# One expert layer, a second buffer for the w2 combinations, the fifth expert's raw sums in SBUF, folding from item 19, attention copies ahead of the weight cast

## The chip, the cores and the metric

One core of one Trainium2 chip. The metric is the device time of one execution in microseconds; the figure before is the median of three runs. TensorE (PE) multiplies and loads weights (PEld), VectorE is DVE, ScalarE is ACT, GpSimd is POOL, and SyncE (SP) issues every DMA of this kernel, all on one queue.

## The reference, cut to what matters

```python
x = chunked_attention(q, k, v)            # 2304 tokens x 512, chunks of 64
P = sinkhorn(exp(x @ w_gate - max))       # 2304 x 8, 8 rounds of row and column norm
for e in range(8):                        # every expert sees every token
    h = relu(x @ w1[e])                   # 512 -> 1024
    out += P[:, e:e+1] * (h @ w2[e])      # 1024 -> 512
h = max(out @ w1, out @ w2, out @ w3)     # second layer, 512 -> 768, with relu
return h @ w_out
```

P is known only when all tokens have been through the attention and the Sinkhorn rounds are over.

## The kernel before, in words

Each fp32 product is made of three matmuls of rounded high and low parts. The tokens are three blocks of 768. The first layer runs over 32 pairs of 128-wide weight blocks per token block ("items" 0 to 31 for block 0, 32 to 63 and 64 to 95 for the others), four items to an expert; the second layer has 27 short items. An item has seven steps (pos 0 to 6), and each step is one Strassen-like product of 6 matmuls into one of three PSUM banks: `pa` (pos 0, 2, 4, 6), `pg` (pos 1 and 5) and `pb` (pos 3). Banks accumulate over the steps of an item.

In block 0 the weights come raw from the inputs. While item n runs, the weight combinations of item n+1 are made for w1 (`prep`, pos 0 and 1) and those of item n for w2 (`prep`, `prep_x`, pos 2 to 5), by ACT (rounding casts), POOL and DVE (remainders). They are used at once and also stored to DRAM (`keep`): the w1 combinations to `w1s` (1792 KB an item, L193), the w2 ones to `w2s` in four stores, of which the two combinations that only later blocks need are `w2x` (L198) and `w2y` (L200), 512 KB each. `w2x` is one place in SBUF (two slots of `wr`) and `w2y` one tile, both reused by every item: the cast that begins the next `w2x` (L182) waits until the store of the last one has landed. Behind L182 and the `w2y` cast (L247) in ACT's queue stand the relu's of pos 4 to 6 (L273), behind the relu of pos 5 stands DVE's remainder (L279), the last reader of bank `pg`, and pos 1 of the next item writes `pg`.

After pos 1, 3 and 5 two down projections of the item before run on PE (L444, 12 matmuls), so an item of block 0 has 42 up and 36 down matmuls. DVE or ACT evicts them. For block 0 the sums of experts 0 to 4 (NRAW = 5) are kept raw: four items into `ar`, then `ar` stored to `up_part` in DRAM, as P is not known. From expert 5 on `ar` takes P-scaled sums, and `fold_all` loads the 30 raw tiles of 256 KB again (`u`, L496) and adds them scaled to `ar` (L499 on DVE), four an item, from item 22.

The attention of the last 12 token tiles is spread over items 0 to 13: scores at pos 6, normalisation at pos 1, values (`att_pv`) at pos 0 of the next item, its copies out of PSUM (L772, PSUM pool `dn`, shared with the down projections) behind ACT's weight cast L247 of that pos; then the store `x_save` at pos 2 and `gate` at pos 4, which takes a buffer of pool `pa` and is evicted by L783. From item 32 on the weights come back from `w1s` and `w2s` through a ring of slots in `wr`.

The order of everything is the order of the code: a table `bg[(n, pos)]` of callbacks (`at`) runs after the step's product, and `prep` runs ahead of the table. SP issues in program order; an issue whose buffer is not free holds all later ones.

Of the kernel before, what the change touches and what calls it, by code (L numbers as in the profile page):

```python
# [9 lines left out]
F32 = mybir.dt.float32  # L10
F32R = mybir.dt.float32r
# [3 lines left out]
AF = mybir.ActivationFunctionType  # L15
ALU = mybir.AluOpType
AX = mybir.AxisListType

P = 128
# [3 lines left out]
DM = H * D  # L23
# [6 lines left out]
KD = DM // P  # L30
SB = 3
TS = NT // SB
W = TS * P // 2
# [5 lines left out]
NRAW = 5  # L39
# [13 lines left out]
def kernel(ctx: ExitStack, tc: tile.TileContext, qk, vv, wg, wts, wts2, out):  # L53
    nc = tc.nc
# [6 lines left out]
    rp = raws.enter_context(tc.tile_pool(name="raw", bufs=1, side="right"))  # L61
# [21 lines left out]
    ar = rg.tile([P, TS, DM], F32, name="ar")  # L83
    xs = dram.tile([NT, P, KD, P], F32, name="xs")
    ys = dram.tile([NT, P, KD, P], F32, name="ys")
    up_part = dram.tile([NRAW, TS, P, DM], F32, name="upart")
    scr = dram.tile([3 * NP2, P, 7, 2, 2, P], F32, name="scr")
    scro = dram.tile([NP2, P, 2, 2, DM], F32, name="scro")
    w1s = dram.tile([NPAIR, P, 7, 512], F32, name="w1s")
# [46 lines left out]

    w1b = lambda n: wr[:, 7 * (n % 2):7 * (n % 2) + 7]
    w2b = lambda n: wr[:, 14 + 4 * (n % 2):18 + 4 * (n % 2)]
    w2x = wr[:, 22:24]

    def prep(n, step):
        if not own(n):
# [15 lines left out]
    def prep_x(n, step):  # L158

        if not own(n):  # L160
            return
        q = lambda c, a: sw[n][:, c].rearrange("p (f a k r) -> p a k f r", a=2, k=2, f=4)[:, a]
        o = lambda x: x.rearrange("p (k f r) -> p k f r", k=2, f=4)
        tt = nc.vector.tensor_tensor
        if step == 0:
            p = wk.tile([P, 2, 256], F32, name="xw", tag="wk")
            s = rp.tile([P, 2, 256], F32, name="w2c", tag="w2c")
            sw2[n] = (p, s)
            for a in range(2):
                nc.scalar.copy(out=o(p[:, a]), in_=q(0, a))  # L170
        elif step == 1:
            p, s = sw2[n]
            w = w2b(n)[:, 0:2]
            tt(out=w[:, :, 1], in0=p, in1=w[:, :, 0].bitcast(F32), op=ALU.subtract)
            tt(out=o(s[:, 0]), in0=q(1, 1), in1=o(p[:, 1]), op=ALU.add)
            tt(out=o(p[:, 1]), in0=q(0, 0), in1=o(p[:, 1]), op=ALU.subtract)
            tt(out=p[:, 0], in0=s[:, 0], in1=p[:, 0], op=ALU.subtract)
            tt(out=o(s[:, 1]), in0=q(1, 0), in1=o(p[:, 0]), op=ALU.subtract)
            sw.pop(n)
        elif step == 2:  # L180
            p, s = sw2[n]
            nc.scalar.copy(out=w2x[:, :, 0], in_=p)  # L182
            y = sums["y", n] = rp.tile([P, 2, 2, 256], F32R, name="w2y", tag="w2y")
            hilo(y[:, :, 0], y[:, :, 1], s)
        else:
            p, s = sw2.pop(n)
            tt(out=w2x[:, :, 1], in0=p, in1=w2x[:, :, 0].bitcast(F32), op=ALU.subtract)

    def keep(n, step):
        f32 = lambda x: x.bitcast(F32).rearrange("p s h f -> p s (h f)")  # L190
        w2o = w2s[n // 2, :, :, n % 2]
        if step == 0:
            nc.sync.dma_start(out=w1s[n], in_=f32(w1b(n)))  # L193
        elif step == 1:
            nc.sync.dma_start(out=w2o[:, 0:1], in_=f32(w2b(n)[:, 0:1]))
            nc.sync.dma_start(out=w2o[:, 5:7], in_=f32(w2b(n)[:, 2:4]))
        elif step == 2:
            nc.sync.dma_start(out=w2o[:, 2:4], in_=f32(w2x))  # L198
        else:
            nc.sync.dma_start(out=w2o[:, 1:5:3], in_=f32(sums.pop(("y", n))))  # L200

# [246 lines left out]
    def new_acc(t):  # L448
        acc[t] = ar[:, t % TS]
        return acc[t]  # L450

    def evict(it, t, p):
        e, pp = it["e"], it["pp"]
        raw = it["sb"] == 0 and e < NRAW
        if raw or it["g"] == 0 or (it["sb"] == 0 and e == NRAW and pp == 0):
            if pp == 0:
                a = new_acc(t)
                if raw:
                    nc.scalar.copy(out=a, in_=p)
                else:  # L460
                    nc.scalar.activation(out=a, in_=p, func=AF.Copy, scale=Pt[:, t, e:e + 1])
            else:
                nc.vector.tensor_tensor(out=acc[t], in0=p, in1=acc[t], op=ALU.add)
                if pp == 3:
                    nc.sync.dma_start(out=up_part[e, t], in_=acc[t])
            return
        nc.vector.scalar_tensor_tensor(
            out=acc[t], in0=p, scalar=Pt[:, t, e:e + 1], in1=acc[t], op0=ALU.mult, op1=ALU.add)
        if it["g"] == NPAIR - 1:
            y_due.append((clock[0], t))  # L470

# [10 lines left out]
    def y_out(t):  # L482
        p = wk.tile([P, KD, P], F32, name="yp", tag="wk")
        for k in range(KD):
            nc.tensor.transpose(p[:, k], acc[t][:, k * P:(k + 1) * P], ident)
        y = acc[t].rearrange("p (k q) -> p k q", k=KD)
        nc.scalar.copy(out=y, in_=p)
        nc.sync.dma_start(out=ys[t], in_=y)

    def fold_all():  # L490
        jobs = [(e, t) for e in range(NRAW) for t in range(TS)]
        got = {}
        for i in range(len(jobs) + 5):
            if i < len(jobs):
                got[i] = big[0].tile([P, DM], F32, name="u", tag="ld", bufs=6)
                nc.sync.dma_start(out=got[i], in_=up_part[jobs[i]])  # L496
            if i >= 5:
                e, t = jobs[i - 5]
                nc.vector.scalar_tensor_tensor(out=acc[t], in0=got.pop(i - 5), scalar=Pt[:, t, e:e + 1],  # L499
                                               in1=acc[t], op0=ALU.mult, op1=ALU.add)  # L500
            yield


    xst = {}

    def x_load(k):
        kind, sb = phases[k]
        if k == 1:
            T = lambda i: big[0].tile([P, 2, W], F32, name=f"xf{i}", tag=f"xf{i}")
        else:  # L510
            T = lambda i: bg_[:, :7 * 2 * W].rearrange("p (i a w) -> p i a w", a=2, w=W)[:, i]
        xst.update({i: T(i) for i in range(7)})
        for i, (q, h) in {5: (1, 0), 0: (0, 0), 2: (1, 1), 1: (0, 1)}.items():
            for j in range(TS // 2):
                t, o = sb * TS + 2 * j + q, xst[i][:, :, j * P:(j + 1) * P]
                nc.sync.dma_start(out=o, in_=(xs if kind == "M" else ys)[t, :, 2 * h:2 * h + 2])
                yield
# [162 lines left out]
    def load_v(t):  # L680
        if t < NT:
            v_t[t] = ap_.tile([P, DM], F32, name="v", tag="v", bufs=3)
            nc.sync.dma_start(out=v_t[t], in_=vv[t])
# [90 lines left out]
    def x_save(t):  # L774
        nc.sync.dma_start(out=xs[t], in_=raw_of(t))
# [56 lines left out]
                              in_=pts[sb - 1, :, q, e].partition_broadcast(P))  # L832


    bg = {}

    def at(n, pos, fn):
        bg.setdefault((n, pos), []).append(fn)
# [5 lines left out]
        at(n, 2, lambda t=t: att_swap(t))  # L844
    for m in range(NT - NPE):
        t, n = NPE + m, 1 + m
        at(n + 1, 0, lambda t=t: (att_pv(t, dn), load_v(t + 3)))
        at(n + 1, 2, lambda t=t: x_save(t))
        at(n + 1, 4, lambda t=t: gate(t, ps_a))
    for t in range(NPE):  # L850
        at(t // 2, 3 + 2 * (t % 2), lambda t=t: gate(t, wk))
    n = NT - NPE + 2
# [13 lines left out]
    def att_close():  # L866
        nonlocal pbm
        att.close()
        pbm = pool("pbm").tile([P, 2, 2, W], F32, name="pbm")
        big[0] = bigs.enter_context(tc.tile_pool(name="big", bufs=1))  # L870

    pbm = bg_ = tq = None
    s3, sr, bigr = ExitStack(), ExitStack(), [None]
# [23 lines left out]

    at(n, 0, att_close)
    for g in range(NPAIR):
        for s_, (a, b) in enumerate(((0, 0), (0, 6), (1, 1), (1, 1))):  # L900
            at(g + a, b, lambda g=g, s_=s_: keep(g, s_))
    decs, folds = [decode_all(i) for i in range(2)], fold_all()

# [4 lines left out]

    for i in range(2):
        at(first_of[2 + i] - 5, 6, lambda i=i: [None for _ in decs[i]])  # L910
    f0 = 4 * NRAW + 2
    for i in range(NRAW * TS + 5):
        at(f0 + i // 4, (0, 2, 4, 6)[i % 4], lambda: next(folds, None))
    for k in range(1, 4):
        n0 = first_of[k]
        g = x_load(k)
        for i in range(13):
            at(*((n + 1 + i // 4, i % 4) if k == 1 else (n0 - 4, i // 2)), lambda g=g: next(g, None))
        for step_ in range(4):
            at(*((n + 5 + step_ // 2, 2 * (step_ % 2)) if k == 1 else  # L920
                 (n0 - 2 + step_ // 3, step_ % 3)), lambda s_=step_: x_sums(s_))
        for pos in range(7) if k == 1 else (0, 2):
            a = 7 * (n0 - 1) + pos + 1
            at(a // 7, a % 7, lambda pos=pos: x_put(pos, 0))
            at((a + 1) // 7, (a + 1) % 7, lambda pos=pos, k=k: x_put(pos, 1, k > 1))
# [21 lines left out]
    with tc.manual_schedule():  # L947
# [43 lines left out]
        for n in range(ni):  # L991
# [3 lines left out]
            for pos in up(n):  # L995
                clock[0] = 7 * n + pos
                if y_due and y_due[0][0] < 7 * n + pos - 1:
                    y_out(y_due.pop(0)[1])
                if pos < 2:
                    prep(n + 1, pos)  # L1000
                elif pos == 2:
                    prep(n, 2)
                    prep_x(n, 0)
                elif pos == 5:
                    prep_x(n, 3)
# [85 lines left out]
```

## Time and profile before

| what | before |
|---|---|
| median of three runs | 1831.68 us (1830.63 to 1832.98) |
| profiled execution | 1831.47 us, its span 1829.7 us |
| PE busy / PEld busy | 1796.5 us / 1704.8 us |
| DVE, ACT, POOL busy | 1314.0, 781.1, 999.3 us |
| DMA | 537.36 MB, 82.6% of 16 engines' span on SP's queue |
| mean granted PE clock | 0.995 of full speed |

PE is nearly always busy, so what counts is where it is not. A matmul's end is modelled in this profile, and neighbours overlap in the rows: six up matmuls start some 1.05 us before the next piece does. Times are from the start of the span; block 0 ends at about 620 us.

### The profile page before, as it was taken

The numbers are of one execution on the slowest core, as the hardware profiler recorded it, in microseconds if no ns is written. First come the engines' busy times: TensorE is split into PE (matmuls) and PEld (weight loads), VectorE is DVE, ScalarE is ACT, GpSimd is POOL, SyncE is SP. The second block draws the span as 40 slices with busy tenths as digits, with TensorE's granted clock in tenths as the row PEclk, the third lists the DMA queues.
The fourth block names the chain that finished last, engine by engine and source line by source line (L and its number), as shares of the span: only waits on it lengthen the run. The fifth ranks groups of instructions, "written<-read, shape, count | busy, mean of one in ns | idle before, by whom it ended". The sixth has DMA issues, their size and how long they took to land.

```text
span 1829.7 us, 30169 instructions
## 1 busy us (share of the span) xinstructions
PE 1796.5 (98%) x10734; PEld 1704.8 (93%) x10740; DVE 1314.0 (72%) x2344; ACT 781.1 (43%) x1574; POOL 999.3 (55%) x894
## 2 busy tenths in 40 slices
PE   7999999999999899999999999999999999999999
PEld 5888888988888899999999999999999999999998
DVE  7666675775887577877888677878888767655535
ACT  5555555555544443343333344333433333333221
POOL 6554555677765667666676577657676655000000
PEclk9999999999999999999999999999999999999999
DMA  6798987989998788989888878988889896877663
GB/s 243 262 342 325 333 303 286 354 316 345 360 333 320 278 308 305 315 285 321 294 312 292 298 273 302 317 287 305 316 308 305 263 319 244 268 254 253 244 248 114
DMA packets 207415, 537.36 MB, mean 294 GB/s; under 512 B 15936, under 2 KB 94880, under 8 KB 182048
## 3 DMA queue, kind: packets, MB, share of 16 engines
q1 hardware_dynamic: 207264, 535.43, 82.6%
q8 instruction: 85, 1.39, 0.3%
q14 instruction: 66, 0.54, 0.1%
HBM read 376.19 MB, written 157.60 MB: 292 GB/s over the span
## 4 chain that ended last, share of the span: by engine, by line
PE 83%; DMA 7%; DVE 4%; issue 2%; ACT 2%; SPq 1%; POOL 1%; POOLq 0%; DVEq 0%; ACTq 0%
PE pa L328 24%; PE dn L386 24%; PE dn L444 14%; PE pg L328 12%; PE pb L328 6%; DMA w2s<-w2y 4%; DMA w2s<-wr 1%; DMA u<-upart 1%; PE gp L782 1%; DMA w1s<-wr 1%; PE s L693 1%; PE xp L770 0%; DVE s L702 0%; DVE hr L279 0%; ACT hr L273 0%
## 5 line engine op out<-in xcount | busy, mean ns | idle before, releaser
L328 PE MATMUL pa<-xh,wr 128*128 128x384 f32 x1824 | 538.8, 338 | 2.9 <-ACT s L335 1.0
L444 PE MATMUL dn<-wr,hr 128*128 128x512 f32 x1476 | 360.2, 395 | 2.6 <-ACT xr L772 2.5
L328 PEld LDWEIGHTS pa<-xh,wr 128*128 128x128 f32 x1824 | 336.1, 188 | 9.5 <-ACT s L335 1.9
L444 PEld LDWEIGHTS dn<-wr,hr 128*128 128x128 f32 x1476 | 276.5, 189 | 60.1 <-ACT xr L772 5.8
L328 PE MATMUL pa<-xl,wr 128*128 128x384 f32 x912 | 306.5, 336 | 2.6 <-DVE xl L541 2.6
L328 PE MATMUL pg<-xh,wr 128*128 128x384 f32 x912 | 274.4, 341 | 12.5 <-DVE hr L279 11.7
L386 PE MATMUL dn<-hr,wr 128*128 128x384 f32 x1344 | 274.2, 334 | 0.0
L335 ACT COPY s<-pa 128x384 f32<-128x384 f32 x246 | 118.6, 482 | 300.5 <-PE pa L328 262.2
L386 PEld LDWEIGHTS dn<-hr,wr 128*128 128x128 f32 x1344 | 236.8, 188 | 0.1
L341 DVE TENSOR_TENSOR c<-pb,s 128x384 f32<-128x384 f32 x82 | 45.7, 558 | 205.7 <-PE pb L328 173.2
L248 POOL TENSOR_TENSOR hr<-c,hr 128x384 fp32r<-128x384 f32 x96 | 110.7, 1159 | 146.0 <-ACT hr L247 140.4
L328 PEld LDWEIGHTS pg<-xh,wr 128*128 128x128 f32 x912 | 168.9, 189 | 16.8 <-DVE hr L279 15.0
L386 PE MATMUL dn<-hx,wr 128*128 128x384 f32 x840 | 180.3, 334 | 0.6 <-DVE ar L395 0.6
L328 PEld LDWEIGHTS pa<-xl,wr 128*128 128x128 f32 x912 | 171.5, 188 | 6.8 <-issue 2.9
L328 PE MATMUL pg<-xl,wr 128*128 128x384 f32 x456 | 153.4, 337 | 0.0
L386 PEld LDWEIGHTS dn<-hx,wr 128*128 128x128 f32 x840 | 148.7, 188 | 1.2 <-DVE ar L395 1.2
L248 POOL TENSOR_TENSOR hr<-tq,hr 128x384 fp32r<-128x384 f32 x128 | 148.2, 1174 | 0.0
L248 POOL TENSOR_TENSOR w2y<-w2c,w2y 128x512 fp32r<-128x512 f32 x32 | 41.6, 1301 | 175.3 <-ACT w2y L247 150.7
L328 PE MATMUL pb<-xh,wr 128*128 128x384 f32 x456 | 134.4, 335 | 0.0
L248 POOL TENSOR_TENSOR hx<-c,hx 128x384 fp32r<-128x384 f32 x60 | 68.5, 1144 | 108.2 <-ACT hx L247 107.0
L395 DVE TENSOR_TENSOR ar<-dn,ar 128x384 f32<-128x384 f32 x240 | 122.6, 546 | 6.8 <-PE dn L386 6.8
L386 PE MATMUL dn<-hy,wr 128*128 128x384 f32 x504 | 111.0, 335 | 0.5 <-DVE ar L395 0.5
(189 smaller groups left out, 3313.3 us busy)
## 6 DMA issues: line engine op xcount, KB each, us to landing
wr<-w2s SPq DMA_DIRECT2D x80, 1024.0 KB, 6.2
w1s<-wr SPq DMA_DIRECT2D x32, 1792.0 KB, 9.1
wr<-w1s SPq DMA_DIRECT2D x54, 1024.0 KB, 7.5
wr<-w1s SPq DMA_DIRECT2D x59, 768.0 KB, 6.8
w2s<-wr SPq DMA_DIRECT2D x64, 512.0 KB, 8.3
wr<-w2s SPq DMA_DIRECT2D x52, 512.0 KB, 6.5
wr<-scr SPq DMA_DIRECT2D x22, 1024.0 KB, 5.0
wr<-scr SPq DMA_DIRECT2D x27, 768.0 KB, 5.8
```

The lines of the kernel that those rows point to most:

```text
L248: (eng or nc.gpsimd).tensor_tensor(out=l, in0=v, in1=h.bitcast(F32), op=ALU.subtract)
L328: nc.tensor.matmul(ps, lhsT=wt[:, x, ws], rhs=y[:, xi, k], start=b not in begun, stop=k == 1 and i == 2, skip_group_check=True)
L335: nc.scalar.copy(out=s[pos], in_=ps)
L341: nc.vector.tensor_tensor(out=inner, in0=ps, in1=s[other], op=ALU.add)
L386: nc.tensor.matmul(p, lhsT=w[:, a, dt * P:(dt + 1) * P], rhs=h[m][:, b], start=m == 0 and q == 0, stop=m == 1 and q == 2)
L395: nc.vector.tensor_tensor(out=o, in0=p, in1=o, op=ALU.add)
L444: nc.tensor.matmul(o, lhsT=h[:, hi, ts], rhs=w, start=(f == 0 and i == 0), stop=(f == 1 and i == 2))
L693: nc.tensor.matmul(ss[g][cs, hp, :], lhsT=a[r, hp, 0, cs], rhs=a[r, hp, 1, cs], start=True, stop=True)
L782: nc.tensor.matmul(p, lhsT=x[:, k, :], rhs=wgr[:, k, :], start=k == 0, stop=k == KD - 1)
```

## The change

- A second place `w2z` for both `w2x` and `w2y` is opened with the pool `big` at item 14; odd items from 15 on use it.
- The stores of `w2x` and `w2y` of item n move from pos 1 to pos 0 of item n+1, and there ahead of the 1792 KB store of `w1s`.
- The raw sums of the fifth expert (e = 4) go to a tile `spare` in SBUF, not to DRAM: 24 stores and 24 loads where there were 30 each.
- `ar` is first written by an ACT copy with P as its scale (six tiles of expert 0, items 19 and 20), then folding adds expert 4 from `spare`, then experts 1 to 3; three jobs an item from item 19, none at pos 4 on DVE. Expert 5's first sums are added by DVE where ACT wrote them.
- The loads of block 1's tokens (`x_load`) move from items 15 to 18 to items 22 to 26, four of their seven tiles lie in `spare`; their sums (`x_sums`) move to items 29 and 30.
- `att_pv` runs ahead of `prep` (table `early`), and `gate` moves from pos 4 to pos 2.

```diff
-    up_part = dram.tile([NRAW, TS, P, DM], F32, name="upart")
+    up_part = dram.tile([NRAW - 1, TS, P, DM], F32, name="upart")
...
-    w2x = wr[:, 22:24]
+    w2z = []
+    w2x = lambda n: w2z[0][:, 0:2] if w2z and n % 2 else wr[:, 22:24]
...
             p, s = sw2[n]
-            nc.scalar.copy(out=w2x[:, :, 0], in_=p)
-            y = sums["y", n] = rp.tile([P, 2, 2, 256], F32R, name="w2y", tag="w2y")
+            x = w2x(n)
+            sums["x", n] = x
+            nc.scalar.copy(out=x[:, :, 0], in_=p)
+            y = w2z[0][:, 2:4] if w2z and n % 2 else rp.tile([P, 2, 2, 256], F32R, name="w2y", tag="w2y")
+            sums["y", n] = y
             hilo(y[:, :, 0], y[:, :, 1], s)
...
-        raw = it["sb"] == 0 and e < NRAW
-        if raw or it["g"] == 0 or (it["sb"] == 0 and e == NRAW and pp == 0):
+        if e < NRAW:
+            a = spare[0][:, t] if e == NRAW - 1 else ar[:, t]
             if pp == 0:
-                a = new_acc(t)
-                if raw:
-                    nc.scalar.copy(out=a, in_=p)
-                else:
-                    nc.scalar.activation(out=a, in_=p, func=AF.Copy, scale=Pt[:, t, e:e + 1])
-            else:
-                nc.vector.tensor_tensor(out=acc[t], in0=p, in1=acc[t], op=ALU.add)
-                if pp == 3:
-                    nc.sync.dma_start(out=up_part[e, t], in_=acc[t])
+                nc.scalar.copy(out=a, in_=p)
+                return
+            nc.vector.tensor_tensor(out=a, in0=p, in1=a, op=ALU.add)
+            if pp == 3 and e < NRAW - 1:
+                nc.sync.dma_start(out=up_part[e, t], in_=a)
             return
...
-        jobs = [(e, t) for e in range(NRAW) for t in range(TS)]
+        jobs = [(e, t) for e in (0, NRAW - 1, *range(1, NRAW - 1)) for t in range(TS)]
+        loads = [j for j in jobs if j[0] != NRAW - 1]
         got = {}
...
+        def load():
+            if loads and len(got) < 6:
+                e, t = loads.pop(0)
+                got[e, t] = big[0].tile([P, DM], F32, name="u", tag="ld", bufs=6)
+                nc.sync.dma_start(out=got[e, t], in_=up_part[e, t])
+
+        for _ in range(5):
+            load()
+        yield
+        for e, t in jobs:
+            load()
+            if e == 0:
+                nc.scalar.activation(out=ar[:, t], in_=got.pop((e, t)), func=AF.Copy, scale=Pt[:, t, e:e + 1])
+            else:
+                u = spare[0][:, t] if e == NRAW - 1 else got.pop((e, t))
+                nc.vector.scalar_tensor_tensor(out=ar[:, t], in0=u, scalar=Pt[:, t, e:e + 1],
+                                               in1=ar[:, t], op0=ALU.mult, op1=ALU.add)
             yield
...
-        at(n + 1, 0, lambda t=t: (att_pv(t, dn), load_v(t + 3)))
-        at(n + 1, 2, lambda t=t: x_save(t))
-        at(n + 1, 4, lambda t=t: gate(t, ps_a))
+        early[n + 1, 0] = lambda t=t: (att_pv(t, dn), load_v(t + 3))
+        at(n + 1, 2, lambda t=t: (x_save(t), gate(t, ps_a)))
...
+        spare.append(big[0].tile([P, TS, DM], F32, name="spare"))
+        w2z.append(big[0].tile([P, 4, 2, 256], F32R, name="w2z"))
...
-        for s_, (a, b) in enumerate(((0, 0), (0, 6), (1, 1), (1, 1))):
+        for s_, (a, b) in enumerate(((0, 0), (0, 6), (1, 0), (1, 0))):
             at(g + a, b, lambda g=g, s_=s_: keep(g, s_))
...
-    f0 = 4 * NRAW + 2
-    for i in range(NRAW * TS + 5):
-        at(f0 + i // 4, (0, 2, 4, 6)[i % 4], lambda: next(folds, None))
+    at(n + 4, 5, lambda: next(folds))
+    for i in range(NRAW * TS):
+        at(n + 5 + i // 3, (0, 2, 4 + 2 * (i >= TS))[i % 3], lambda: next(folds, None))
...
-            at(*((n + 1 + i // 4, i % 4) if k == 1 else (n0 - 4, i // 2)), lambda g=g: next(g, None))
+            at(*((n + 8 + i // 5 + 2 * (i >= 9), i % 5) if k == 1 else (n0 - 4, i // 2)),
+               lambda g=g: next(g, None))
...
+                if (n, pos) in early:
+                    early[n, pos]()
                 if pos < 2:
                     prep(n + 1, pos)
```

In the changed kernel the source lines are numbered otherwise (L193 is L198 there, L198 is L203, L200 is L205, L182 is L185, L273 is L278, L772 is L788). On SP's queue, at the start of item 28, after the loads of the raw weights `st`, there stood:

```order
L119 DMA st<-in_wts 128x512
L120 DMA st<-in_wts 128x2x256
L193 DMA w1s<-wr 128x3584
L496 DMA u<-upart 128x512
L198 DMA w2s<-wr 128x2x512
L200 DMA w2s<-w2y 128x2x512
```

and in the changed kernel, at the same place:

```order
L119 DMA st<-in_wts 128x512
L120 DMA st<-in_wts 128x2x256
L203 DMA w2s<-w2z 128x2x512
L205 DMA w2s<-w2z 128x2x512
L198 DMA w1s<-wr 128x3584
L847 DMA pbm<-pts 128x3x128 x2
```

The two stores of item 27's combinations now come from `w2z` and stand ahead of the `w1s` store, and no `u` load is left here.

On ACT, at the start of an attention item (`s<-pa` and `s<-pg` are the copies behind pos 0 and pos 1, `xr<-xp` those of the attention values), before:

```order
L703 ACTIVATE s<-s 128x256 x2
L335 COPY s_2770<-pa 128x384
L247 CAST wr<-st 128x3x256
L772 COPY xr<-xp 128x4x64 x2
L335 COPY s_2811<-pg 128x384
```

and now:

```order
L719 ACTIVATE s<-s 128x256 x2
L340 COPY s_2770<-pa 128x384
L788 COPY xr<-xp 128x4x64 x2
L252 CAST wr<-st 128x3x256
L340 COPY s_2813<-pg 128x384
```

The two copies change places with the cast.

On ACT in item 19 of the changed kernel, from the cast that begins the odd item's `w2x` to the relu of pos 6:

```order
L185 CAST w2z<-xw 128x2x256
L252 CAST w2z<-w2c 128x2x256
L278 ACTIVATE hr<-c 128x384
L280 ACTIVATE c<-c 128x384
L508 ACTIVATE ar<-u,Pt 128x512
L278 ACTIVATE hr<-pg 128x384
```

where before stood:

```order
L182 CAST wr<-xw 128x2x256
L247 CAST w2y<-w2c 128x2x256
L273 ACTIVATE hr<-c 128x384
L275 ACTIVATE c<-c 128x384
L273 ACTIVATE hr<-pg 128x384
```

The casts have another target, and a scaled copy of expert 0 stands ahead of the relu of pos 5.

## Rows read from the trace of the kernel before

**Rows 1.** The page: the span, and busy time by engine.

```profile
span 1829.7 us, 30169 instructions
PE 1796.5 (98%) x10734; PEld 1704.8 (93%) x10740; DVE 1314.0 (72%) x2344; ACT 781.1 (43%) x1574; POOL 999.3 (55%) x894
```

**Rows 2.** Busy time in stretches: engines, granted clock, DMA share, GB/s.

```profile
450.00:500.00 50.00, 48.83 (x241) 43.20 (x240) 42.63 (x67) 24.43 (x49) 34.98 (x28) 1.00 0.98 366
500.00:550.00 50.00, 48.53 (x241) 43.15 (x240) 42.18 (x68) 25.45 (x50) 36.11 (x28) 1.00 0.96 340
550.00:600.00 50.00, 43.71 (x209) 38.44 (x207) 32.94 (x55) 21.71 (x44) 24.59 (x18) 0.95 0.84 328
650.00:700.00 50.00, 50.00 (x290) 50.00 (x289) 37.64 (x63) 22.71 (x47) 36.47 (x37) 1.00 0.89 301
```

**Rows 3.** Waits of PE over the span: us in total, times, longest.

```profile
PE pg L328 <- DVE hr L279: 11.7, 8, 4.8
...
PE dn L444 <- ACT xr L772: 2.5, 4, 0.9
...
PE pa L328 <- ACT Pt L783: 0.8, 2, 0.6
```

**Rows 4.** Waits of ACT over the span, those of L182 on DMA.

```profile
ACT wr L182 <- DMA w2s<-wr: 73.8, 17, 7.3
```

**Rows 5.** Timeline of ACT, items 29 and 30: start, duration, idle before.

```profile
559.62 0.59 ACT L182 CAST wr<-xw 128x512 fp32r<-128x512 f32 x1 [7.26 <-DMA w2s<-wr]
560.85 0.62 ACT L247 CAST w2y<-w2c 128x512 fp32r<-128x512 f32 x1 [0.64 <-DMA w2s<-w2y]
...
563.45 0.86 ACT L247 CAST wr<-st 128x768 fp32r<-128x768 f32 x1
...
576.99 0.59 ACT L182 CAST wr<-xw 128x512 fp32r<-128x512 f32 x1 [3.83 <-DVE w2c L178]
```

**Rows 6.** Chain that ended last, in order of time: start, us, piece.

```profile
230.07 3.02 PE dn L444 x12
...
549.69 1.04 PE pb L328 x6
...
563.47 1.34 PE pg L328 x6
564.81 4.33 PE dn L444 x12
...
571.22 2.76 PE dn L444 x12
...
601.51 2.29 PE pg L328 x6
603.79 3.64 PE dn L444 x12
```

**Rows 7.** Busy time in stretches behind the two longest waits, columns as rows 2.

```profile
563.00:567.00 4.00, 3.53 (x12) 3.07 (x13) 3.17 (x5) 1.79 (x4) 3.92 (x5) 0.71 0.99 417
601.00:605.00 4.00, 3.49 (x10) 3.20 (x11) 1.58 (x3) 3.29 (x6) 4.00 (x4) 0.50 1.01 394
```

**Rows 8.** Timeline of SP's queue, item 28: start and duration of an issue.

```profile
547.03 0.37 SPq L193 DMA_DIRECT2D w1s<-wr  x1
...
549.06 0.87 SPq L198 DMA_DIRECT2D w2s<-wr  x1
```

**Rows 9.** Line L198 (stores of w2x), 440 to 600 us: issue to landing.

```profile
DMA to landing us min/median/max: 9.3/10.0/14.7
```

**Rows 10.** Line L193 (stores of w1s), 440 to 580 us: issue to landing.

```profile
DMA to landing us min/median/max: 8.9/10.3/11.0
```

**Rows 11.** Timeline of ACT at the start of an attention item.

```profile
228.90 0.84 ACT L247 CAST wr<-st 128x768 fp32r<-128x768 f32 x1
229.63 0.66 ACT L772 COPY xr<-xp 128x256 f32<-128x256 f32 x2
```

**Rows 12.** The page, DMA issues: KB each, median us to landing.

```profile
u<-upart SPq DMA_DIRECT2D x30, 256.0 KB, 8.8
```

More of the change, by code (lines that the diff above doesn't have):

```diff
@@ L186, in prep_x @@
             p, s = sw2.pop(n)
-            tt(out=w2x[:, :, 1], in0=p, in1=w2x[:, :, 0].bitcast(F32), op=ALU.subtract)
+            x = sums["x", n]
+            tt(out=x[:, :, 1], in0=p, in1=x[:, :, 0].bitcast(F32), op=ALU.subtract)
     def keep(n, step):
@@ L197, in keep @@
         elif step == 2:
-            nc.sync.dma_start(out=w2o[:, 2:4], in_=f32(w2x))
+            nc.sync.dma_start(out=w2o[:, 2:4], in_=f32(sums.pop(("x", n))))
         else:
@@ L453, in evict @@
         e, pp = it["e"], it["pp"]
-        raw = it["sb"] == 0 and e < NRAW
-        if raw or it["g"] == 0 or (it["sb"] == 0 and e == NRAW and pp == 0):
+        if e < NRAW:
+            a = spare[0][:, t] if e == NRAW - 1 else ar[:, t]
             if pp == 0:
-                a = new_acc(t)
-                if raw:
-                    nc.scalar.copy(out=a, in_=p)
-                else:
-                    nc.scalar.activation(out=a, in_=p, func=AF.Copy, scale=Pt[:, t, e:e + 1])
-            else:
-                nc.vector.tensor_tensor(out=acc[t], in0=p, in1=acc[t], op=ALU.add)
-                if pp == 3:
-                    nc.sync.dma_start(out=up_part[e, t], in_=acc[t])
+                nc.scalar.copy(out=a, in_=p)
[3 more added lines that the diff above has]
+                nc.sync.dma_start(out=up_part[e, t], in_=a)
             return
         nc.vector.scalar_tensor_tensor(
-            out=acc[t], in0=p, scalar=Pt[:, t, e:e + 1], in1=acc[t], op0=ALU.mult, op1=ALU.add)
+            out=ar[:, t], in0=p, scalar=Pt[:, t, e:e + 1], in1=ar[:, t], op0=ALU.mult, op1=ALU.add)
         if it["g"] == NPAIR - 1:
@@ L484, in y_out @@
         for k in range(KD):
-            nc.tensor.transpose(p[:, k], acc[t][:, k * P:(k + 1) * P], ident)
-        y = acc[t].rearrange("p (k q) -> p k q", k=KD)
+            nc.tensor.transpose(p[:, k], ar[:, t, k * P:(k + 1) * P], ident)
+        y = ar[:, t].rearrange("p (k q) -> p k q", k=KD)
         nc.scalar.copy(out=y, in_=p)
@@ L490, in fold_all @@
     def fold_all():
-        jobs = [(e, t) for e in range(NRAW) for t in range(TS)]
+        jobs = [(e, t) for e in (0, NRAW - 1, *range(1, NRAW - 1)) for t in range(TS)]
+        loads = [j for j in jobs if j[0] != NRAW - 1]
         got = {}
[L493 to L500, printed above, removed]
+        def load():
[14 more added lines that the diff above has]
+                                               in1=ar[:, t], op0=ALU.mult, op1=ALU.add)
             yield
+    spare = []
     xst = {}
@@ L508, in x_load @@
         if k == 1:
-            T = lambda i: big[0].tile([P, 2, W], F32, name=f"xf{i}", tag=f"xf{i}")
+            xf = spare[0].rearrange("p t d -> p (t d)").rearrange("p (i a w) -> p i a w", a=2, w=W)
+            T = lambda i: (xf[:, (1, 3, 4, 6).index(i)] if i in (1, 3, 4, 6) else
+                           big[0].tile([P, 2, W], F32, name=f"xf{i}", tag=f"xf{i}"))
         else:
@@ L832, in p_load @@
                               in_=pts[sb - 1, :, q, e].partition_broadcast(P))
-    bg = {}
+    bg, early = {}, {}
     def at(n, pos, fn):
@@ L917 @@
         for i in range(13):
-            at(*((n + 1 + i // 4, i % 4) if k == 1 else (n0 - 4, i // 2)), lambda g=g: next(g, None))
+            at(*((n + 8 + i // 5 + 2 * (i >= 9), i % 5) if k == 1 else (n0 - 4, i // 2)),
+               lambda g=g: next(g, None))
         for step_ in range(4):
-            at(*((n + 5 + step_ // 2, 2 * (step_ % 2)) if k == 1 else
+            at(*((n + 15 + step_ // 2, 2 * (step_ % 2)) if k == 1 else
                  (n0 - 2 + step_ // 3, step_ % 3)), lambda s_=step_: x_sums(s_))
```

## The prediction

> **What bounds the kernel now.** I read the page first, then busy time in stretches, then the waits of PE and of ACT, then the timelines around the longest waits, and last the chain. PE is busy 1796.5 of 1829.7 us [rows 1], so at most 33 us can be won without less PE work, and the change removes no matmul. From 650 us on, in the later blocks, PE is busy all of a stretch at full clock [rows 2]: time won before is kept to the end. What PE lacks in block 0's second half is 1.17, 1.47 and 6.29 us in three stretches of 50 us [rows 2], while the DMA engines are 98, 96 and 84% busy. The list of waits names the cause: PE waits 11.7 us in 8 pieces, the longest 4.8, for DVE's remainder L279 to let go of bank `pg`, and 3.3 us in 6 pieces in the attention items for ACT's copies L772 and L783 [rows 3].
>
> L279 is only the last link. In ACT's queue the relu that it needs stands behind L182, and L182 waited for the store of the last `w2x` 17 times, 73.8 us in all [rows 4]. In item 29 it began at 559.62 after 7.26 us, and the `w2y` cast behind it had 0.64 us more to wait; in item 30, where the store was in time, ACT was idle 3.83 us until DVE had made the input [rows 5]. So 3.83 us is what that place costs anyway, and the store made item 29 about 3.4 us worse; PE's `pg` then began at 563.47 [rows 6].
>
> **The change part by part.**
>
> *Second buffer, earlier stores.* The store of `w2x` takes 9.3 to 14.7 us to land, median 10.0 [rows 9], and in item 28 it was issued 2.0 us behind the 1792 KB store of `w1s` [rows 8]. Odd items from 15 now write `w2z`, even ones a place last read two items ago, some 31 us, against at most 14.7 us of landing. L182 and the cast behind it then wait for DVE alone, as in item 30, and all eight `pg` waits should go: 11.7 us [rows 3].
>
> A wait costs more than its idle time. Six matmuls behind one take 1.34 us on the chain against 1.04 [rows 6]: 0.30 more, times 8, is 2.4 us.
>
> Two waits also cost clock. Before the wait that ended at 563.47 and the one that ended at 601.51 the clock was at its full level, 2.4 GHz; behind them the stretch means were 0.71 and 0.50 of it, the latter being 1.2 GHz [rows 7]. Twelve down matmuls took 4.33 and 3.64 us there instead of 2.76, and the six ahead of the second 2.29 instead of 1.34 [rows 6]: 1.57 + 0.88 + 0.95 = 3.4 us, which come back with the waits.
>
> *Attention.* The copies L772 stood behind a cast; the row behind the cast's start begins 0.73 us later [rows 11]. That covers most of the longest such wait, 0.9 us, and the four together are 2.5 us [rows 3]. Moving `gate` to pos 2 puts its copy L783 ahead of L182, which ends the other 0.8 us. Refilling PE costs 0.26 a wait here (3.02 against 2.76 for twelve down matmuls [rows 6]), 1.6 for six. Bounds: 4.9 us if all goes, nothing if something else in ACT's queue holds the copies as long; with the `w2x` stores landing earlier too I take 4.0, near the upper end, because both waits stand directly behind what is moved away.
>
> *The fifth expert in SBUF.* Six stores and six loads of 256 KB fall away, 3.1 MB, no PE time by themselves. DVE's count of folds falls from 30 to 24, but six first sums of expert 5 come to it from ACT, so DVE is even. What helps is that pos 4, where DVE has L279's chain, has no fold now: counted at nothing, since item 30 with one there had no wait.
>
> *Six scaled copies on ACT.* They are new on the path that ends in L279. A cast of the same 128x512 size takes 0.59 us [rows 5]. Two of the six stand between L182 and the relu of pos 5 (items 19 and 20); the first may also wait for its load, whose landing took 8.8 us in the median [rows 12]. It is issued only at pos 5 of the item before, behind the `sw` load, so up to some 4 us late, but there ACT holds only copies that PE needs from pos 4 on, 6 us later. Bounds 0 and 0.6 x 2 + 1; I take 1.0 us as loss. Behind the first copy on ACT stands the weight cast of pos 1, for which POOL waits; POOL is 55% busy [rows 1] and takes that.
>
> *Later `x_load`, `x_sums`.* The sums stand in items 29 and 30 where two folds stood; `spare` is read by folds until item 22 and loaded from item 25, so no wait. In item 31 the casts of block 1's tokens share ACT with the relu's; by the times behind L182 there PE would be late by 0.1 to 0.5 us, taken as 0.2.
>
> *`w1s` stores behind the pair.* 1 MB more is ahead of them, at 340 GB/s [rows 2] 3.1 us. Their landing of 8.9 to 11.0 us [rows 10] becomes 12 to 14. The cast that overwrites their source came 16.4 us after the issue in item 28 (547.03 [rows 8], 563.45 [rows 5]), 13.0 without the 3.4 us of that item's wait. So the cast may come up to 1 us late in the worst item. ACT's idle time before L182, 3.83 us [rows 5], covers that: nothing now, up to 1 us an item if that cover is gone.
>
> *Pace of the DMA engines.* By the sizes in the code an item moves 4.72 MB, with four `u` loads 5.77, with three 5.51; items 23 and 26, with `x_load` beside, 5.8 and 5.9. Undisturbed an item is 3 x 2.76 + 7 x 1.05 = 15.6 us [rows 6], which asks for 353 to 377 GB/s; the rows show 366 over 50 us [rows 2] and 394 to 417 over 4 us [rows 7]. I count nothing for it: an excess of 3% over two items is half a microsecond an item, less than any slack above. The Trainium skill, page "DMA: Bandwidth & Descriptors", section "Specifications", gives about 358 GB/s as the HBM limit of a core. The stretch at 366 does not agree with it as a ceiling; by it items 23 and 26 would run 0.5 and 0.9 us over and the sum would be 1.4 us higher.
>
> *Sum.* 11.7 + 2.4 + 3.4 + 4.0 - 1.0 - 0.2 = 20.3 us. The profiled execution took 1831.47 us, 1.8 more than its span, and the median of the runs is 1831.68, so no correction is due: 1831.5 - 20.3 = **1811.2 us**.
>
> **The rivals.**
>
> A. The transfers become the bound and one wait replaces the other. For it: shares of 96 to 98% [rows 2]. If the engines yield 340 GB/s and no more, an item of 5.5 to 5.9 MB needs 16.2 to 17.3 us, and loads of raw weights come late instead of stores. Then what PE lacked from 450 to 600 us, 8.9 us, stays: 1820.1. Against it: ACT's list shows no wait of its weight casts for loads, and less is moved than before. The rule of about 358 GB/s named above points this way; the 366 of the rows speaks against it.
>
> B. The attention part gives nothing, because the copies are held by the scores' exponentials ahead of them: 1815.2.
>
> C. The buffer does not matter, since DVE is the real holder of L182 (it was in item 30). Then only the attention part comes, less the losses: 1828.7. Against it: item 30 waited for DVE and PE did not wait for `pg` afterwards.
>
> D. Slower: the `w1s` store, now behind 1 MB more, holds the cast at pos 0 in every item, at 1 us of PE for each us beyond ACT's idle time. To turn a gain of 20.3 into a loss over 31 items it must exceed that by 0.65 us an item, so land 13.0 + 3.8 + 0.65 = 17.5 us after issue against my 12 to 14; at 18.5 us it would give 1842. Against it: the longest landing now is 11.0.
>
> **How the numbers follow.** Main case 0.60, A 0.15, B 0.14, C 0.06, D 0.05. The forecast is the main case's. Without the losses and with the whole attention part it is 1809.1, and waits too short for the list may add some 2 us (an estimate): 1807 is the lower end. The upper end takes in B and A: 1821. About 0.2% (3.7 us) is what a measurement here can tell from no change. Faster by more: main, A, B and a little of C, 0.90; within it: 0.05; slower: 0.05.
>
> **What would show it.** In the profile after: no wait of PE's `pg` for L279's line over 0.5 us; ACT's waits for `w2s` stores gone from item 16 on, those for DVE left at about 4 us; clock 1.00 between 550 and 620 us; the attention copies gone from PE's list; the wait for block 1's first `tq` unchanged. A shows as DMA share 1.0 with ACT or POOL waiting for `st` or `sw`; D as ACT waiting for `w1s`. I would be wrong if ACT's new copies in items 19 and 20 hold PE for more than 2 us, or if the eighth wait, at 601.51, has its cause in the token casts rather than in L182.

## The result and the profile after

The changed kernel takes **1806.69 us** in the median (1805.21 to 1807.04), the kernel before 1831.62 beside it; the ratio is 0.9862 with a 95% interval of 0.9845 to 0.9879. That is 24.9 us less where 20.3 were forecast, and 0.3 us below the lower end of the range. The profiled execution took 1807.0 us, its span is 1805.2.

The head of the page, as in [rows 1]:

```profile
span 1805.2 us, 30137 instructions
PE 1789.3 (99%) x10734; PEld 1704.0 (94%) x10740; DVE 1304.9 (72%) x2344; ACT 781.2 (43%) x1574; POOL 1000.1 (55%) x894
```

Busy time in stretches, columns and first three stretches as in [rows 2]:

```profile
450.00:500.00 50.00, 50.00 (x251) 45.05 (x250) 40.67 (x70) 26.93 (x53) 36.97 (x29) 1.00 0.96 353
500.00:550.00 50.00, 50.00 (x252) 45.23 (x251) 40.58 (x67) 26.61 (x52) 38.85 (x31) 1.00 0.88 325
550.00:600.00 50.00, 50.00 (x262) 45.09 (x261) 31.27 (x53) 26.38 (x52) 31.75 (x23) 1.00 0.78 302
```

PE is busy all of these 150 us, at full clock. Its list of waits, longest sums first, no longer has L284 (L279 before), L788 (L772) or L799 (L783), which were [rows 3]:

```profile
PE xp L776 <- ACT aT L742: 1.9, 3, 0.9
PE tp L741 <- DVE e L730: 1.6, 2, 1.4
PE warm L963 <- DVE wones L966: 1.5, 1, 1.5
PE pa L333 <- DVE c L346: 1.3, 2, 0.7
...
PE pg L333 <- DVE tq L302: 0.7, 1, 0.7
```

ACT's waits at L185 (L182 before) over the span; [rows 4] was 73.8 us in 17:

```profile
ACT wr L185 <- DVE w2c L179: 78.1, 19, 5.3
ACT w2z L185 <- DVE w2c L179: 30.7, 9, 4.1
...
ACT wr L185 <- DMA w2s<-wr: 0.7, 1, 0.7
```

Issue to landing, first of the `w2x` stores from 430 to 590 us ([rows 9]: median 10.0), then of the `w1s` stores from 430 to 570 us ([rows 10]: 10.3):

```profile
DMA to landing us min/median/max: 5.2/6.0/8.6
```

```profile
DMA to landing us min/median/max: 9.3/10.6/11.9
```

The `w2x` store lands 4 us sooner; the `w1s` store, now behind it, 0.3 us later in these windows (e9 below compares two kernels that differ in the order alone).

**Where the time came from.** PE's timeline has one product into `pb` in each item, at pos 3; the starts of these products measure the items to some hundredths. Before, the first matmul of `pb` in items 1, 14, 17, 32 and 35:

```profile
56.31 0.33 PE L328 MATMUL pb<-xh,wr 128*128 128x384 f32 x1
306.34 0.33 PE L328 MATMUL pb<-xh,wr 128*128 128x384 f32 x1
354.78 0.42 PE L328 MATMUL pb<-xh,wr 128*128 128x384 f32 x1
608.34 0.33 PE L328 MATMUL pb<-xh,wr 128*128 128x384 f32 x1
646.57 0.33 PE L328 MATMUL pb<-xh,wr 128*128 128x384 f32 x1
```

After:

```profile
56.11 0.33 PE L333 MATMUL pb<-xh,wr 128*128 128x384 f32 x1
300.15 0.33 PE L333 MATMUL pb<-xh,wr 128*128 128x384 f32 x1
348.59 0.42 PE L333 MATMUL pb<-xh,wr 128*128 128x384 f32 x1
584.26 0.33 PE L333 MATMUL pb<-xh,wr 128*128 128x384 f32 x1
622.54 0.33 PE L333 MATMUL pb<-xh,wr 128*128 128x384 f32 x1
```

The differences grow from 0.20 to 6.19, stay at 6.19, go to 24.08 and stay at 24.03: 5.99 us come from the attention items, none from items 15 to 17, 17.89 from items 18 to 32. "Item i" here means from `pb` of item i-1 to `pb` of item i. The wait at pos 1 of item 30 (3.0 us, the one that ended at 563.47 in [rows 6]) makes item 30 long, and so on. Because up to item 1 kernels with nearly the same code differ by up to 2.4 us (`pb` of item 1 starts at 54.2 to 56.6 us in the thirteen traces), the experiments are read from item 1 to item 35: 590.26 us before, 566.43 after, **23.8 us** gained. The medians of four runs cannot tell 1 us apart; the items can, but only within the one execution that was profiled. That execution was the fastest of ten for e4 and the slowest of four for e11, so a wait that differs from one execution to the next stands in the last column as it fell there.

### The profile page after: what moved, and what is told of

It reads as the page before. It is cut to its first block, busy times and chain, and to the rows that moved or that the text cites. A ratio compares the mean times of both kernels' runs of the same rounds, so it can differ in the third digit from the quotient of the medians.

```text
span 1805.2 us, 30137 instructions
## 1 busy us (share of the span) xinstructions
PE 1789.3 (99%) x10734; PEld 1704.0 (94%) x10740; DVE 1304.9 (72%) x2344; ACT 781.2 (43%) x1574; POOL 1000.1 (55%) x894
## 4 chain that ended last, share of the span: by engine, by line
PE 94%; DVE 3%; issue 1%; ACT 1%; SPq 0%; DMA 0%; POOLq 0%; POOL 0%; DVEq 0%; ACTq 0%
PE pa L333 28%; PE dn L391 25%; PE dn L449 19%; PE pg L333 14%; PE pb L333 7%; PE gp L798 1%; PE s L709 1%; PE xp L786 1%; DVE s L718 0%; DVE xT L557 0%; PE warm L963 0%; SPq L412 0%; DMA xr<-ys 0%; DVE nm L717 0%; DVE tq L302 0%
## 5 line engine op out<-in xcount | busy, mean ns | idle before, releaser
L400 DVE TENSOR_TENSOR ax<-dn,ax 128x384 f32<-128x384 f32 x180 | 92.6, 550 | 17.8 <-PE dn L391 17.8
## 6 DMA issues: line engine op xcount, KB each, us to landing
w1s<-wr SPq DMA_DIRECT2D x32, 1792.0 KB, 10.7
```

The lines of the kernel that those rows point to most:

```text
L400: nc.vector.tensor_tensor(out=o, in0=p, in1=o, op=ALU.add)
```

## The experiments

Beside them the kernel before took 1831.6 to 1831.7 us.

| kernel | median, us | ratio, 95% interval | gain from item 1 to 35, us |
|---|---|---|---|
| changed kernel | 1806.7 | 0.9845 to 0.9879 | 23.8 |
| e1: stores' order alone | 1811.2 | 0.9868 to 0.9901 | 18.8 |
| e2: second buffer alone | 1814.9 | 0.9893 to 0.9922 | 15.6 |
| e3: attention alone | 1830.1 | 0.9986 to 1.0006 | 0.6 |
| e4: fifth expert alone | 1829.8 | 0.9978 to 0.9997 | 3.9 |
| e5: changed, without second buffer | 1806.9 | 0.9850 to 0.9879 | 23.8 |
| e6: order + gate at pos 2 | 1810.6 | 0.9868 to 0.9898 | 19.7 |
| e7: order + values early | 1808.7 | 0.9863 to 0.9903 | 22.7 |
| e8: changed, without fifth expert | 1807.3 | 0.9854 to 0.9883 | 22.8 |
| e9: as e5, stores behind `w1s` | 1816.8 | 0.9902 to 0.9937 | 14.1 |
| e10: changed, 512 KB more an item | 1806.4 | 0.9845 to 0.9875 | 23.6 |
| e11: changed, 1 MB more an item | 1807.9 | 0.9856 to 0.9887 | 20.1 |

**e1, the stores' order alone.** The kernel before with

```diff
-        for s_, (a, b) in enumerate(((0, 0), (0, 6), (1, 1), (1, 1))):
+        for s_, (a, b) in enumerate(((0, 0), (0, 6), (1, 0), (1, 0))):
```

> The kernel before with the w2x and w2y stores moved to pos 0 ahead of the w1s store, and one place for w2x as before. Between the two traces the w2x store's landing fell from 9.7 to 5.9 us in the median (longest 14.7 and 8.6), and from its issue to the next L182 there are 11 us or more. Theory 1, the store's place in the queue does it alone: the waits for w2s at L182 nearly vanish (under 5 us in total), PE's pg waits for L279 fall from 11.7 to under 1 us, and the time falls by 17.5 to 18.1 us, to about 1813.7. Theory 2, that of the prediction, the second buffer does it: half or more of the pg waits stay, and the time is 1823 or more.

It does most of it: 18.8 of 23.8 us, with one place for `w2x`. Its landings from 440 to 600 us have a median of 6.2 us. One wait is left, in item 30, and it comes from a late issue: the `w2x` store of item 28 was issued 17.6 us after `pb` of that item (10.6 in the changed kernel), at 541.28, and landed at 548.39, when L182 had waited 3.6 us for it. The longest landing, 10.3 us, is that of the next store, and L182 behind that one waited for DVE. From PE's list and ACT's:

```profile
PE pg L328 <- DVE hr L279: 2.0, 1, 2.0
```

```profile
ACT wr L182 <- DVE w2c L178: 93.6, 28, 4.4
ACT wr L182 <- DMA w2s<-wr: 4.4, 2, 3.6
```

Theory 1 held, with one `pg` wait of 2.0 us where it gave under 1, and by the medians the gain is 20.5 us, 2.4 more than it gave. What neither theory had: the waits of the attention items went too. Items 1 to 14 gave 4.06 us here, and L772 and L783 are no longer in PE's list, though no attention code had moved. The list of weight loads (PEld) still has a short rest:

```profile
PEld dn L444 <- ACT xr L772: 2.7, 11, 0.3
```

Before, the same row read

```profile
PEld dn L444 <- ACT xr L772: 5.8, 11, 1.3
```

**e2, the second buffer alone.** The kernel before with `w2z` and the lambda `w2x` of the change, the stores at pos 1 behind `w1s`.

> The kernel before with the second place for w2x and w2y alone, from item 15 on, the stores where they were. With two items (31 us) between reuses and landings of 9 to 15 us both theories of the waits expect the pg waits after item 15 gone: 17.5 to 18 us less, about 1813.8. If that and the run with the stores' order alone both give it, either edit is enough and the other is spare. A third theory, that the w1s store or DVE is the holder: ACT still waits over 5 us for DVE at L182 and the time stays above 1825.

Items 18 to 32 are free of waits here too (16.9 us of the 17.89), so for these items either edit is enough. The buffer exists from item 14 on only, and items 1 to 14 still wait: `dn` for the attention copies (L777 there) 4.0 us in 4, where the kernel before had 2.5. By the medians it is 3.7 us behind e1.

**e3, the attention part alone.** The kernel before with table `early` for `att_pv` and `gate` at pos 2.

> The kernel before with the attention part alone: values ahead of the weight casts, gate at pos 2. Between the two traces the pb of pos 3 came 6.0 us earlier over items 2 to 14, of which 13 items gave 0.15 us each whether or not they had a wait. Theory 1: the waits and their refill are 4.0 and the gate's new place gives 0.15 us an item of itself, in all 6.0 us: 1825.6. Theory 2, the prediction's sum: 4.0 us, 1827.6, and items without a wait stay at 18.98 us.

Both theories failed: 0.6 us, or 1.6 by the medians, whose interval takes in no change. Items 4, 5, 7, 8, 11 and 12 went to 18.82 to 18.87 us, but items 6, 9 and 10 took 19.90, 19.68 and 19.51, since L182 still waited for stores in this stretch. ACT's waits at L182 from 60 to 290 us in this kernel:

```profile
ACT wr L182 <- DVE w2c L178: 36.3, 8, 5.3
ACT wr L182 <- DMA w2s<-wr: 15.8, 4, 5.2
```

Items 1 to 14 gave 2.5 us, and items 18 to 32 took 2.0 back, most of it in item 30, 24.23 us against 20.49: the same late store, this time with L182 waiting 9.7 us and `pg` 6.2.

**e4, the fifth expert alone.** The changed kernel with one place for `w2x`, the stores at pos 1 behind `w1s`, values and gate where they were.

> The kernel before with the fifth expert in SBUF alone, with the new folds, scaled copies and later token loads; one place for w2x, stores and attention as before. The prediction's step: no PE time by itself, less 1.2 for the copies and the casts: 1832 to 1833, and the eight pg waits stay within 2 us of 11.7. Rival: 3.1 MB less and no fold at pos 4 land the w2x store earlier in items 22 to 31, so some of those waits shrink: the pg waits sum to 4 to 9 us and the time falls by 4 to 10 us.

Neither the prediction's step nor the rival held: five `pg` waits are left, 9.2 us in all, and the time falls by 1.9 us by the medians. There is a trade inside: item 20 became 6.4 us longer (22.17 against 15.73), items 22 to 32 together 8.9 us shorter. SP's queue in item 18 shows why item 20 lost:

```profile
377.50 0.37 SPq L125 DMA_DIRECT2D sw<-in_wts  x1
377.97 2.32 SPq L500 DMA_DIRECT2D u<-upart  x5
...
383.38 0.72 SPq L198 DMA_DIRECT2D w1s<-wr  x1
384.59 0.33 SPq L500 DMA_DIRECT2D u<-upart  x1
385.31 0.37 SPq L203 DMA_DIRECT2D w2s<-wr  x1
```

The folding opens with five loads in one burst; the `w2x` store behind them and behind `w1s` took 11.5 us to land, L185 waited 7.3 for it, and PE's `pg` 3.7. With the stores early (e5) the same burst costs nothing: item 20 takes 15.73.

**e5, the changed kernel without the second buffer.** The line that opens `w2z` is left out.

> The changed kernel without the second buffer: w2x and w2y in one place, all else as changed. The run with the stores' order alone kept one pg wait of 2.0 us (item 30, where the w2x store was issued late and took 10.3 us); otherwise its items 15 to 31 were free of waits for stores. Theory 1, the buffer is spare: 1806.7 to 1807.5 us, items 15 to 31 within 0.1 us of those of the changed kernel. Theory 2, it is still needed in the one or two items where SP issues late: one pg wait of 2 to 3 us with its refill, 1809 us. The prediction's reading, that the buffer is what removes the waits: 1820 us or more.

Theory 1: items 14 to 32 are those of the changed kernel within 0.03 us each, the gain is 23.8 us, the median 0.2 us away. In the changed kernel the buffer is spare.

**e6 and e7, which attention edit.** The stores' order of e1 with `gate` at pos 2, and with `att_pv` ahead of `prep`, one each.

> The kernel before with the stores' order and gate at pos 2, values still behind the casts. With the order alone items 4 to 12 took 18.98 us each without a wait. Theory 1, 0.15 us an item belongs to the gate's place: 18.83 us in these items, 1811.2 less 2.0 = 1809.2. Theory 2, it belongs to the values ahead of the casts: 18.98, 1811.2.

> The kernel before with the stores' order and the values ahead of the casts, gate at pos 4. Theory 1: nothing is left for it to remove once the stores are early; 18.98 us in items 4 to 12 and 1811.2 in all. Theory 2, it carries the 0.15 us: 18.83 and 1809.2.

I had the two edits the wrong way round. With `gate` moved, items 4 to 12 take 18.97 to 19.00 us as in e1 (its 0.9 us over e1 is a shorter wait in item 30); with the values early, 18.82 to 18.83. The short `PEld` row above stands in e6 too, unchanged at 2.7 us in 11, and is gone in e7. Over items 1 to 14 e1 gives 4.06, e6 4.12 and e7 6.00 us: the values early are worth 1.9 us, the gate's place nothing.

**e8, the changed kernel without the fifth expert's part.** The kernel before with second buffer, order, values and gate.

> The kernel before with everything of the change but the fifth expert's part: second buffer, stores' order, values early, gate at pos 2; five raw experts in DRAM and four folds an item from item 22. The runs with the order alone and the buffer alone took 15.75 to 15.77 us in items 24 to 31 against 15.64 in the changed kernel, where the fold at pos 4 is gone. Theory 1: 0.11 to 0.13 us in eight items, in all 0.9 us, is all that part gives: 1807.6 us. Theory 2, fewer bytes matter as well: a wait of PE's pg over 0.5 us is back in items 22 to 31 and the time is 1810 or more.

Theory 1: items 24 to 31 take 15.74 to 15.77 us, 15.64 in the changed kernel: 0.98 us in all. The rows show the cause in item 26: DVE's fold at pos 4, DVE's last reader of `pg`, and the weight load of pos 1 (from the timelines of DVE and PEld):

```profile
481.43 0.74 DVE L504 SCALAR_TENSOR_TENSOR ar<-u,Pt,ar 128x512 f32<-128x512 f32 x1
...
483.81 0.55 DVE L284 SCALAR_TENSOR_TENSOR hr<-pg,hr 128x384 fp32r<-128x384 f32 x1
```

```profile
484.07 0.19 PEld L333 LDWEIGHTS pa<-xh,wr 128*128 128x128 f32 x1
484.41 0.19 PEld L333 LDWEIGHTS pg<-xh,wr 128*128 128x128 f32 x1
```

L284 ends at 484.36 and the load of `pg` starts 0.05 us later, 0.34 after the one ahead of it where 0.17 is usual. DVE has no idle time between the rows shown, so the fold's 0.74 us moves L284 back. e8's lists of waits do not have it; PEld's list in e1 has the same delay as a rest of 0.15 us at pos 1 of items 24 to 29 and 31.

**e9, the place behind `w1s`.** e5 with the two loops exchanged, so that `w1s` is issued first at pos 0:

```diff
-    for g in range(NPAIR):
-        for s_, (a, b) in enumerate(((0, 0), (0, 6), (1, 0), (1, 0))):
+    for s_, (a, b) in enumerate(((0, 0), (0, 6), (1, 0), (1, 0))):
+        for g in range(NPAIR):
```

> The changed kernel without the second buffer, as in the run of 1806.9 us, but with the w2x and w2y stores at pos 0 behind the w1s store and no longer ahead of it. Theory 1, it is the 1792 KB ahead that made them late: landings go back to 9 to 10 us in the median, L182 waits for w2s in six or more items, the attention items have waits again and the time is 1811 to 1822 us. Theory 2, the earlier place at pos 0 does it alone, since the next L182 comes 11 us after the issue: no pg wait over 0.5 us and 1806.9 us.

Theory 1, for the time and for the landing: first the `w2x` stores of e5 from 250 to 640 us, then those of e9:

```profile
DMA to landing us min/median/max: 5.0/5.6/9.2
```

```profile
DMA to landing us min/median/max: 5.1/9.7/11.8
```

The `w1s` stores go the other way, a median of 10.7 us in e5 and 9.2 in e9. ACT's and PE's lists in e9 show the old rows again:

```profile
ACT wr L185 <- DMA w2s<-wr: 31.9, 8, 6.6
```

```profile
PE pg L333 <- DVE hr L284: 3.4, 2, 3.1
PE dn L449 <- ACT xr L788: 2.2, 4, 0.8
```

9.7 of the 23.8 us hang on which of the two stores is issued first: 4.0 in the attention items, 5.1 in items 18 and 20, only 0.6 in items 21 to 32. The long wait is in item 20 again, behind the burst of five loads. Items 21 to 32 gave 16.2 us here, of 16.8 in e5, though the stores stand behind `w1s` and land in 9 to 10 us; with the stores at pos 1 behind `w1s` (e4, whose attention part is that of before) they gave 8.9. So in these items it is mostly the earlier step, pos 0 in place of pos 1, that counts: L185 begins 10.7 us (median of items 14 to 30) after the issue, and most stores land just in time. How much the earlier step gives in the kernel before by itself, with five experts in DRAM, no run shows.

**e10 and e11, the pace of the DMA engines.** The changed kernel with stores that nobody needs, at pos 3 of the item behind; e10 has the first line only:

```diff
+            nc.sync.dma_start(out=dup[n, :, 0:2], in_=f32(sums["x", n]))
+            nc.sync.dma_start(out=dup[n, :, 2:4], in_=f32(sums["y", n]))
...
+    for g in range(15, 31):
+        at(g + 1, 3, lambda g=g: keep(g, 4))
```

> The changed kernel with one more store of w2x (512 KB) to an unused tensor at pos 3 of the item behind, for items 15 to 30; nothing of the outputs is touched. By the sizes items 16 to 18 move 5.2 MB and items 19 to 31 up to 6.0. If 366 GB/s, the most that a stretch of 50 us showed, is the ceiling, an item takes up to 16.5 us, 0.8 more, about 9 us in all: 1816. If the engines can give the 394 to 417 GB/s seen over 4 us, 6.0 MB fit into 15.64 us: 1807 to 1808.

> As the run with one more store, with w2y too: 1 MB more an item, up to 6.6 MB in items 19 to 31. At a ceiling of 366 GB/s 17.9 us an item, 2.3 more in some eleven items: 25 to 30 us, 1835. At 417 GB/s 15.7 us: 1807 to 1810.

512 KB more an item cost nothing that shows. 1 MB cost 3.8 us by the items, nearly all in item 30 (19.36 us), and 1.2 us by the medians; the profiled execution, 1810.4 us, is the slowest of its four, the others took 1807.3 to 1808.1. Stretches of e11, columns as before:

```profile
400.00:450.00 50.00, 50.00 (x251) 45.14 (x250) 41.39 (x70) 25.71 (x50) 35.01 (x27) 1.00 1.05 413
450.00:500.00 50.00, 50.00 (x252) 45.16 (x251) 40.64 (x69) 27.47 (x54) 37.76 (x30) 1.00 1.04 406
500.00:550.00 50.00, 48.08 (x236) 43.14 (x235) 39.26 (x64) 24.66 (x48) 35.78 (x27) 0.98 0.98 385
```

413 GB/s over 50 us with PE busy all the time: the 366 before was what the kernel asked for, not a ceiling. But 1 MB more is where transfers begin to be late. ACT's list in e11 has

```profile
ACT wr L157 <- DMA sw<-in_wts: 13.5, 6, 5.4
ACT wr L256 <- DMA w1s<-wr: 9.9, 6, 2.7
```

in items 25 to 30, where e10 has neither; the wait of 5.4 us, for a load of raw weights, is the one in item 30.

The Trainium skill gives about 358 GB/s as a core's HBM limit ("DMA: Bandwidth & Descriptors", section "Specifications"); its page "HBM Reference", section "Specifications (TRN2)", says that a core streaming alone measures about 425. This kernel runs on one core, and the 413 agrees with the second.

## Why the prediction was off

By its own terms, with the marks above:

- **The `pg` waits, their refill and the clock (11.7 + 2.4 + 3.4, less 0.2 in item 32): right, the size in part by luck.** Forecast 17.3; the eight items concerned (18, 22, 24, 25, 26, 28, 30, 32) gave 1.06, 0.90, 0.47, 0.63, 0.97, 1.65, 4.85 and 6.72, in all 17.25. Each small one is its wait plus 0.30, and the two long ones bear out the price of the clock. Item 32 keeps 15.85 us against 15.62 of its neighbour, the 0.2 charged for the token casts. But in items 24, 25, 26, 28 and 30 the change also took away the fold at pos 4, some 0.12 us each by e8; without these 0.6 us the waits gave 16.6, 0.7 less than forecast.
- **The fold at pos 4 (counted at nothing): 1.0.** The reason given was that item 30 with a fold there had no wait; it had one, too short for PE's list. e8 puts it at 0.98 us over items 24 to 31: the 0.6 above, and nearly 0.4 of the next point.
- **Short waits: left out of the sum.** Items 27, 29 and 31 gave 0.39, 0.14 and 0.11 without a row in PE's list: 0.64, of which only some 0.3, in item 27, is a wait for the store. "Some 2 us" for such stood in the lower end only.
- **Attention (4.0): the size was off, and its upper bound (4.9) was wrong.** The span from item 1 to 14 gave 5.99. The listed waits with their refill are 4.06 of it, as e1 shows; the other 1.9 are short waits for L772 that cost PE 0.15 us in items with no row in PE's list. PEld's list, which the prediction does not use, had them: 5.8 us in 11 where PE's had 2.5 in 4. That the 4.0 met the 4.06 so closely is partly luck: items 4, 6, 8 and 10, which held the six listed waits, are 3.9 us longer before than in e1 for 3.3 us of waits, so a refill costs about 0.1 us a wait there and not 0.26.
- **Six scaled copies (-1.0): nothing.** Items 19 and 20 take 15.96 and 15.73 us before and after. A copy takes 0.72 us, more than the 0.59 used in the sum, and none waits for its load. The copy that the prediction charged, between L185 and the relu of pos 5, does delay L284 in item 19; but `pg` was free long before PE needed it. Before, L279 and the first weight load of `pg`:

```profile
397.30 0.56 DVE L279 SCALAR_TENSOR_TENSOR hr<-pg,hr 128x384 fp32r<-128x384 f32 x1
398.58 0.19 PEld L328 LDWEIGHTS pg<-xh,wr 128*128 128x128 f32 x1
```

After, the copy, L284 and the same load:

```profile
389.54 0.71 ACT L508 ACTIVATE ar<-u,Pt 128x512 f32<-128x512 f32 x1
390.66 0.56 DVE L284 SCALAR_TENSOR_TENSOR hr<-pg,hr 128x384 fp32r<-128x384 f32 x1 [0.55 <-ACT hr L278]
391.33 0.19 PEld L333 LDWEIGHTS pg<-xh,wr 128*128 128x128 f32 x1
```

The bank was free 0.72 us before the load, and now 0.11 us: the copy used up the slack, no more.

- **The rest:** 0.20 up to item 1 and 0.42 behind item 32 (the thirteen traces lie between 1220.8 and 1221.5 us there) are of the size of what traces differ by without a cause in the change. 17.25 + 0.64 + 5.99 + 0.62 = 24.5 us, the difference of the spans.

So the step that failed in the sum is the reading of which delays cost PE time, from PE's list alone: 2.0 too little for the attention, 1.0 for the fold at pos 4 put at nothing, 1.0 of loss for copies that only used up slack. Against them stand 0.7 too much for the `pg` waits, 0.3 of a short wait and the 0.6 of the rest: 20.3 becomes 24.5. The lower end of the range stood on 4.9 for the attention, no losses and 2 us of short waits, 24.4 us in all, so it was missed by less than the runs scatter (1805.2 to 1807.0). That the time fell just outside is chance; that it lies 4 us below the forecast is not.

**The mechanism was right about the holder and wrong about the edit.** L182 waiting for the `w2x` store was the cause, but I gave the cure to the second buffer and, beside some help for the attention, saw in the new order of the stores only a cost for `w1s`. The order alone does 18.8 us (e1), and the buffer adds nothing to the changed kernel (e5). The order has two parts, the place ahead of `w1s` and the step from pos 1 to pos 0: e9 puts the first at 9.7 us in the changed kernel without the buffer, and there items 21 to 32 owe most to the second. I also read the attention waits as the work of the cast just ahead; e3, where that cast was out of the way, kept three of the four (1.4 us), and e1, where it was not, lost them: L182 held these copies as well.

**The rivals.** A, the pace: refuted for the changed kernel, which moves 353 GB/s from 400 to 500 us where e10 moves 389 without loss; in e11, at up to 413, A's sign appears, ACT waiting for `sw`. B, no gain from attention: refuted, though e3 alone looks like it. C, DVE as the real holder: DVE does hold L185 now, 3.7 us an item (66.2 in 18 from 300 to 640 us), and that costs PE nothing. D, `w1s` as the new holder: its landing went from 10.3 to 10.6, not to 12 to 14; ACT has no wait for it in the changed kernel (in e11 it has).

**Of the signs named ahead,** all stand in the profile after: no `pg` wait for L284, the clock at 1.00 from 550 us on, the copies gone from PE's list, the wait for block 1's first `tq` still 0.7.

The parts over items 1 to 35: stores' order 18.8, values early 1.9, fifth expert (no fold at pos 4) 1.0, and 2.1 for the last wait in item 30 (17.90 us in e1, 15.76 in its neighbours). That last part is not a fixed size: item 30 took 17.90, 17.02 and 15.90 us in e1, e6 and e7, which have the same code from item 15 on, each with the `w2x` store of item 28 issued 5 to 7 us later behind `pb` than in the changed kernel. With the buffer (e8), where that issue is as late, or with the fifth expert's part, where it is early (e5), the wait is gone. The order and the values together, a handful of lines, reach 1808.7 us (e7). No run was clearly faster than the changed kernel. What the clock's part would be by itself was not tried.

## What to carry to other kernels

When a buffer is reused late because a store is slow, look first at what stands ahead of that store in its queue: issuing it earlier, and ahead of a bigger one that nobody waits for, may do as much as a second buffer, and needs no memory. A wait is charged to the last link (here DVE's L279 or ACT's copies), so follow it back until one instruction explains all places, and expect edits to the links alone to do little while it stands. Waits too short for PE's list still cost 0.1 to 0.2 us an item: compare the length of items with and without the neighbour in question, and read the list of weight loads too.

## What was not expected of the hardware

The 16 DMA engines gave 413 GB/s over 50 us beside a PE that was busy all the time (e11), with a busy share above 1.0; the share of 0.96 to 0.98 before was therefore no sign of a limit. The order of two stores issued within some 2 us of each other decided 4 us of landing for the smaller one (medians of 5.6 us ahead and 9.7 behind, e5 and e9), while the larger one landed in 10.7 us behind it and 9.2 ahead of it.
